# Hourglass attention then a quick-GELU layer on one Trainium2 core: GpSimd's order of work over v, q and k, two moves placed earlier, one load placed later

## The chip, the cores and the metric

The kernel runs on one core of one Trainium2 chip. The metric is the time of one execution on the device in microseconds (us). The engines are named as in the profile: PE (TensorE, matrix products; PEld is its weight load), DVE (VectorE), ACT (ScalarE), POOL (GpSimd) and SP (SyncE, which here only issues DMAs; POOL issues DMAs too). Each engine takes its own instructions strictly in order, and semaphores hold an instruction until what it needs is done.

## The reference, cut to what matters

Batch 8, 8 heads, 576 positions, head dimension 64. Two attentions are added: one over means of four neighbouring positions (its output is repeated four times), and one over the full sequence in which a position sees only positions less than 4 away. The result, as 4608 tokens of 512, goes through a 512 to 2048 to 512 layer.

```python
q_d = q.reshape(B, H, Sd, factor, D).mean(axis=3)      # factor = 4; k_d, v_d alike
out_up = np.repeat(sm_attn(q_d, k_d, v_d), factor, axis=2)
mask = np.abs(pos[:, None] - pos[None, :]) < factor
scores = np.where(mask, scale * np.matmul(q, k.transpose(0, 1, 3, 2)), -1e9)
out_local = np.matmul(softmax(scores), v)
x = (out_up + out_local).transpose(0, 2, 1, 3).reshape(B * S, H * D)
h = x @ w_in
return (h * (1.0 / (1.0 + np.exp(-1.702 * h)))) @ w_out
```

## The kernel before, in words

The order of every engine is written out by hand: an instruction stands on its engine where the Python code records it, and nothing reorders it. The main loop (line 1062) runs over 9 groups of 512 tokens. Group g computes the layer for its tokens: `mm1` (64 products at line 866 and a Silu on ACT at line 877), then `mm2` (64 products at line 930, output through `osb` at line 915). Into the same PE stream it weaves the attention of batch b = g + 1, whose result `xT` the next group reads. The places are counted in steps (line 959): a dictionary `steps` holds functions to call before a given product; steps 0 to 15 lie in `mm1`, step n from 16 on lies before product n - 16 of `mm2`. Functions with the same step run in the order in which they were added.

The heads of a batch are treated in two quads, qd 0 and 1. Per batch, in order:

- `load_qk` (line 201): POOL issues four DMAs, k and q of each quad, from float32 in memory to bfloat16 on chip. The buffers are double. `load_v` (ten DMAs from SP, float32, one buffer `vf`) and `load_v4` (twelve DMAs from SP into one buffer `v4`, four for each of three chunks) bring v in two layouts.
- `prep_qk` (line 298): DVE transposes k and q (line 270) into `kT` and `qT`. From batch 3 (`WIDE` = 3) on, the layout is turned so that 64 rows serve one head: `keep_odd` (line 278) has POOL copy the odd halves of k and q, and `swap` has DVE make eight moves for each quad (line 286, one 32 x 576 piece each): two that overwrite the odd half of k, two that put the kept half in its place, then the same for q. The names below: k even, k odd, q even, q odd, each two moves.
- `pool_qk` (line 316): POOL sums four neighbouring positions of k, then of q (lines 322 and 326) into `kdT` and `qdT`, for the coarse scores.
- `prep_v4` (line 342): POOL sums four neighbouring values of v, a pair of instructions (lines 346 and 349) for each of three chunks, into `vd`. `prep_vx` (line 334): POOL casts `vf` to `vb`, three instructions (lines 336 and 338).
- On PE: `s_pe(0)` at step 13 and `s1` at step 34 (local scores, line 455, then coarse scores, line 464; these read `kdT` and `qdT`), and the AV products of the quads (line 809, `av_t`) at steps 44 and 58, 13 or 14 products apart. AV writes the three PSUM tiles `PA`; `normalise_t` (line 813) then takes logarithms and exponentials of the denominators on ACT (lines 821, 822), multiplies on DVE into `xT` (lines 827, 842), and adds the coarse part: on POOL for quad 0, on DVE for quad 1 (both line 836).

The code that places all this for b >= 3 is lines 1096 to 1109, and the steps are lines 1117 to 1124. In program order of batch b >= 3, POOL has before the change: sums of quad 0's k and q, the odd copies of quad 1, `v4` chunk 0, sums of quad 1's k and q, `v4` chunks 1 and 2, the four loads of batch b + 2 (while b < 6), then, from the steps, the odd copies of quad 0 of batch b + 1, the two adds of line 836, and the three casts of `vf` for batch b + 1.

Of the kernel before, what the change touches and what calls it, by code (L numbers as in the profile page):

```python
# [19 lines left out]
def kernel(  # L20
# [9 lines left out]
    nc = tc.nc  # L30
    B, H, S, D = q.shape
    SD = S // 4
    HP = H // 2
    NQ = H // 4
# [5 lines left out]
    WIDE = 3  # L40
# [147 lines left out]
    def load_1(name, src, store, b, qd):  # L188
        t = ldp.tile(
            [128, 1152], BF16, name=f"{name}b{qd}", tag=f"{name}b{qd}", bufs=2  # L190
        )
        nc.gpsimd.dma_start(
            out=t,
            in_=bass.AP(
                tensor=src.tensor, offset=src[b, 4 * qd].offset,
                ap=[[1152, 128], [1, 1152]],
            ),
        )
        store[b, qd] = t

    def load_qk(b, qd):
        load_1("k", k, kf, b, qd)
        load_1("q", q, qf, b, qd)
# [17 lines left out]
    def load_vb(b, i):  # L221
        for par in range(2):
            nc.gpsimd.dma_start(  # L223
                out=vbs[b % 2][64 * par : 64 * par + 64, i, :, 0:D],
                in_=bass.AP(
                    tensor=v.tensor,
                    offset=v[b, 0].offset + (114 * i + KSTART[par]) * D,
                    ap=[[D, 64], [S * D, H], [1, D]],
                ),
            )  # L230

    def load_v4(b):
        for kc in range(3):
            for u in range(2):
                for qd in range(NQ):
                    nc.sync.dma_start(
                        out=v4[64 * u : 64 * u + 48, kc, 2 * qd : 2 * qd + 2],
                        in_=bass.AP(
                            tensor=v.tensor,
                            offset=v[b, 4 * qd + u].offset + kc * 48 * 4 * D,  # L240
                            ap=[[4 * D, 48], [(3 - 2 * u) * S * D, 2], [1, 4 * D]],
                        ),
                    )
# [10 lines left out]
    def load_w_out(c):  # L254
        nc.gpsimd.dma_start(
            out=w_out_bf[:, 4 * c : 4 * c + 4, :],
            in_=bass.AP(
                tensor=moe_w_out.tensor, offset=moe_w_out.offset + c * 512 * d_model,
                ap=[[d_model, 128], [128 * d_model, 4], [1, d_model]],
            ),  # L260
        )


    qT, kT, qdT = {}, {}, {}
# [11 lines left out]
    odd = {}  # L276

    def keep_odd(b, qd):
        for name, src in (("k", kT), ("q", qT)):
            t = work.tile([128, S], BF16, name="odd", tag="odd")  # L280
            nc.gpsimd.tensor_copy(out=t, in_=src[b, qd][:, :, 1])  # L281
            odd[name] = t

    def move(dst, src):
        with nc.allow_low_precision("a sum of one element each"):
            nc.vector.tensor_reduce(  # L286
                out=dst, in_=src[:, :, None], axis=mybir.AxisListType.X, op=ALU.add
            )

    def swap(b, qd):  # L290
        for name, src in (("k", kT), ("q", qT)):
            tt = src[b, qd]
            for p in (0, 64):
                move(tt[p : p + 32, :, 1], tt[p + 32 : p + 64, :, 0])
            for p in (0, 64):
                move(tt[p + 32 : p + 64, :, 0], odd[name][p : p + 32])

    def prep_qk(b, qd):
        prep_1("k", b, qd)
        prep_1("q", b, qd)  # L300
# [6 lines left out]
    def reduce_qk(b, qd, name):  # L307
        t = kdT[qd][:, 0:SD, :] if name == "k" else new_qdT(b, qd)
        src = (kT if name == "k" else qT)[b, qd]
        with nc.allow_low_precision("the sum is rounded once, as the pairwise one is"):  # L310
            nc.vector.tensor_reduce(
                out=t, in_=src.rearrange("p (j f) a -> p j a f", f=4),
                axis=mybir.AxisListType.X, op=ALU.add,
            )

    def pool_qk(b, qd, names="kq"):
        for name, src in (("k", kT), ("q", qT)):
            if name not in names:
                continue
            sv = src[b, qd].rearrange("p (j f) a -> p j f a", f=4)  # L320
            t1 = work.tile([128, SD, 2, 2], FP32, name="pq", tag="pq")
            nc.gpsimd.tensor_tensor(  # L322
                out=t1, in0=sv[:, :, 0:2, :], in1=sv[:, :, 2:4, :], op=ALU.add
            )
            dst = kdT[qd][:, 0:SD, :] if name == "k" else new_qdT(b, qd)
            nc.gpsimd.tensor_tensor(
                out=dst, in0=t1[:, :, 0, :], in1=t1[:, :, 1, :], op=ALU.add
            )
# [5 lines left out]
    def prep_vx(b):  # L334
        x, y = vf[b], vbs[b % 2]
        nc.gpsimd.tensor_copy(out=y[:, :, 0::2, 0:D], in_=x[:, :, 0::2])
        for p in (0, 64):
            nc.gpsimd.tensor_copy(
                out=y[p : p + 64, :, 1::2, 0:D], in_=x[64 - p : 128 - p, :, 1::2]
            )  # L340

    def prep_v4(b, eng, kcs=range(3)):
        for kc in kcs:
            x = v4[0:112, kc].rearrange("p h (f d) -> p h f d", f=4)
            t1 = work.tile([128, HP, 2, D], FP32, name="v2", tag="v2")
            eng.tensor_tensor(  # L346
                out=t1[0:112], in0=x[:, :, 0:2, :], in1=x[:, :, 2:4, :], op=ALU.add
            )
            eng.tensor_tensor(
                out=vds[b % 2][0:112, kc, :, 0:D],  # L350
                in0=t1[0:112, :, 0, :], in1=t1[0:112, :, 1, :], op=ALU.add,
            )


    def flat(p):
        return p.rearrange("p x n -> p (x n)")
# [516 lines left out]
    def new_gT():  # L873
        return moe_sb.tile([128, n_ffc, TG], BF16, name="gT", tag="gT")
# [90 lines left out]
    def after(src, eng):  # L965
        return lambda t: eng.tensor_copy(out=t, in_=src)
# [95 lines left out]
    for g in range(n_groups):  # L1062
        b = g + 1
        if g == 0:
            load_vb(1, 0)
            load_vb(1, 1)
            prep_qk(1, 0)
            pool_qk(1, 0)
            prep_qk(1, 1)
            load_vb(1, 2)  # L1070
            load_vb(1, 3)
            load_vb(1, 4)
            load_w_out(2)
            load_w_out(3)
            reduce_qk(1, 1, "q")
            reduce_qk(1, 1, "k")
            for qd in range(NQ):
                load_qk(2, qd)
            nc.gpsimd.memset(v4[32:64], 0.0)
            for x, c in ((0, 1.0), (1, 4.0)):  # L1080
                nc.vector.memset(ones[:, x, :], c)
            load_v(2, gate=after(w_out_bf[0:1, 12, 0:1], nc.gpsimd))
            load_v4(2)
        elif b < WIDE:
            for p in (0, 64):
                nc.vector.tensor_copy(out=mask[p : p + 64, 1], in_=mask[64 - p : 128 - p, 0])
            prep_qk(b, 0)
            pool_qk(b, 0)
            for qd in range(NQ):
                load_qk(b + 1, qd)  # L1090
            prep_vx(b)
            load_v(b + 1)
            prep_qk(b, 1)
            pool_qk(b, 1)
            prep_v4(b, nc.gpsimd)
        elif b < B:
            if b + 1 < B:
                load_v(b + 1)
            swap(b, 0)
            pool_qk(b, 0)  # L1100
            prep_qk(b, 1)
            keep_odd(b, 1)
            swap(b, 1)
            prep_v4(b, nc.gpsimd, (0,))
            pool_qk(b, 1)
            prep_v4(b, nc.gpsimd, (1, 2))
        if 1 < b < B - 2:
            for qd in range(NQ):
                load_qk(b + 2, qd)
        steps = {}  # L1110
        if b < B:
            pos = POS_G.get(g, POS)
            for n, f in zip(pos, attention(b, None if g else (1, 2))):
                steps.setdefault(n, []).append(f)
            if g == 0:
                steps.setdefault(VDP_0, []).append(lambda: prep_vd_pe(1, flat(PA[2])))
            if g and b + 1 < B:
                for n, f in (
                    (17, lambda: prep_qk(b + 1, 0)),
                    (17, lambda: keep_odd(b + 1, 0)),  # L1120
                    (45, lambda: prep_vx(b + 1)),
                    (32, lambda: load_v4(b + 1)),
                ):
                    steps.setdefault(n, []).append(f)
        gT = new_gT() if g else gT0
        mm1(g, gT, steps, 0 if g else 6)
        mm2(g, gT, {n - 16: f for n, f in steps.items() if n >= 16})
# [30 lines left out]
```

## Time and profile before

| quantity | value |
| --- | --- |
| median of 3 runs | 314.78 us (314.07 to 315.19) |
| the profiled execution's own time | 315.07 us |
| its span (first to last instruction) | 313.0 us, so 2.1 us lie outside it |
| PE busy | 295.1 us |
| DVE, ACT, POOL busy | 184.5, 208.9, 176.8 us |
| granted PE clock | full in every slice |
| group 2, first product to that of group 3 | 34.20 us |
| groups 3, 4, 5 | 32.28, 32.26, 32.28 us |
| group 6 | 32.59 us |

PE is the engine that is busy nearly all the time, so what counts is where it waits. A table of busy shares does not show that; the list of PE's waits and its timeline do. Groups 2 to 6 carry the batches (3 to 7) in the turned layout, which is where the change works. Times in the text are from the start of the span unless counted from a group's first product at line 866.

### The profile page before, as it was taken

The numbers are of one execution on the slowest core, as the hardware profiler recorded it, in microseconds if no ns is written. First come the engines' busy times: TensorE is split into PE (matmuls) and PEld (weight loads), VectorE is DVE, ScalarE is ACT, GpSimd is POOL, SyncE is SP. The second block draws the span as 40 slices with busy tenths as digits, with TensorE's granted clock in tenths as the row PEclk, the third lists the DMA queues.
The fourth block names the chain that finished last, engine by engine and source line by source line (L and its number), as shares of the span: only waits on it lengthen the run. The fifth ranks groups of instructions, "written<-read, shape, count | busy, mean of one in ns | idle before, by whom it ended". The sixth has DMA issues, their size and how long they took to land.

```text
span 313.0 us, 8666 instructions
## 1 busy us (share of the span) xinstructions
PE 295.1 (94%) x3620; PEld 148.9 (48%) x3663; DVE 184.5 (59%) x343; ACT 208.9 (67%) x349; POOL 176.8 (56%) x212
## 2 busy tenths in 40 slices
PE   7789999999999969998999999998999899999995
PEld 3455455445544435444544454445444544444444
DVE  5883526812787986997699869986996340000000
ACT  5556781867886767668866887688769686316611
POOL 8764690299829799379938894777577500000000
PEclk9999999999999999999999999999999999999999
DMA  6999999899799669823983299417100110010011
GB/s 133 155 197 209 172 118 208 164 197 276 153 233 229 133 149 215 205 42 99 208 233 70 74 201 246 89 49 174 68 2 35 38 67 2 34 67 36 0 67 67
DMA packets 64646, 40.01 MB, mean 128 GB/s; under 512 B 44640, under 2 KB 56032, under 8 KB 64608
## 3 DMA queue, kind: packets, MB, share of 16 engines
q0 software_dynamic: 18336, 14.81, 34.0%
q1 hardware_dynamic: 45600, 24.46, 30.2%
q8 instruction: 28, 0.46, 0.7%
q10 hardware_dynamic: 672, 0.20, 0.3%
q14 instruction: 10, 0.08, 0.1%
HBM read 44.83 MB, written 9.44 MB: 173 GB/s over the span
## 4 chain that ended last, share of the span: by engine, by line
PE 45%; DVE 23%; POOL 14%; issue 6%; ACT 5%; DMA 5%; SPq 1%; POOLq 0%; ACTq 0%
PE pm L930 18%; PE pm L866 15%; DVE kT L286 9%; DVE qT L286 9%; POOL v L346 5%; POOL pq L322 4%; PE pa L866 3%; PE pa L809 2%; DMA qb<-in_q_dram 2%; DVE xT L827 2%; ACT r L821 2%; ACT r L822 2%; PE pa L930 2%; DVE xT L836 2%; DMA vb<-in_v_dram 2%
## 5 line engine op out<-in xcount | busy, mean ns | idle before, releaser
L866 PE MATMUL pm<-xT,w_in_bf 128*128 128x512 bf16 x496 | 118.2, 379 | 1.6 <-ACT xT L669 0.5
L930 PE MATMUL pm<-w_out_bf,gT 128*128 128x512 bf16 x505 | 114.6, 379 | 3.3 <-issue 3.2
L877 ACT ACTIVATE gT<-pm 128x512 bf16<-128x512 f32 x128 | 76.3, 598 | 41.9 <-PE pm L866 41.9
L866 PEld LDWEIGHTS <-w_in_bf 128*128 128x128 bf16 x576 | 55.6, 98 | 67.2 <-issue 1.1
L930 PEld LDWEIGHTS <-gT 128*128 128x128 bf16 x560 | 52.8, 98 | 62.1 <-issue 0.5
L497 DVE TENSOR_TENSOR es<-es,mask 128x600 bf16<-128x600 bf16 x28 | 22.4, 820 | 25.6 <-ACT es L483 25.0
L827 DVE TENSOR_TENSOR xT<-pa,r 128x300 bf16<-128x300 f32 (+3 forms) x96 | 24.1, 304 | 21.3 <-ACT r L822 16.9
L915 ACT ACTIVATE osb<-pm 128x512 f32<-128x512 f32 (+2 forms) x35 | 20.2, 580 | 24.0 <-PE pm L930 18.4
L917 DVE TENSOR_SCALAR osb<-pm 128x128 f32<-128x128 f32 x1 | 0.3, 292 | 55.5 <-ACT osb L915 55.5
L322 POOL TENSOR_TENSOR pq<-kT 128x576 f32<-128x576 bf16 x13 | 14.9, 1146 | 28.3 <-DVE kT L286 18.0
L821 ACT ACTIVATE r<-pa 128x504 f32<-128x504 f32 (+1 forms) x36 | 20.6, 573 | 11.9 <-PE pa L809 11.9
L346 POOL TENSOR_TENSOR v<-v 112x512 f32<-112x512 f32 x18 | 24.5, 1359 | 0.0
L270 DVE STREAM_TRANSPOSE kT<-kb 128x576 f32<-128x576 f32 x16 | 20.0, 1252 | 6.0 <-DMA kb<-in_k_dram 5.8
L322 POOL TENSOR_TENSOR pq<-qT 128x576 f32<-128x576 bf16 x14 | 16.3, 1167 | 12.5 <-DVE qT L286 12.3
L483 ACT ACTIVATE es<-pa 128x600 bf16<-128x600 f32 x32 | 19.7, 668 | 5.1 <-PE pa L401 5.0
L822 ACT ACTIVATE r<-r 128x504 f32<-128x504 f32 (+1 forms) x36 | 22.2, 617 | 1.1
L270 DVE STREAM_TRANSPOSE qT<-qb 128x576 f32<-128x576 f32 x16 | 19.8, 1240 | 0.5 <-DMA qb<-in_q_dram 0.4
L866 PE MATMUL pa<-xT,w_in_bf 128*128 128x512 bf16 x63 | 19.6, 379 | 0.0
L286 DVE TENSOR_REDUCE kT<-kT 32x576 bf16<-32x576 bf16 x20 | 15.9, 793 | 3.5 <-POOL odd L281 3.1
L223 POOL DMA_DIRECT2D vb<-in_v_dram x18 | 12.3, 698 | 9.3 <-DMA w_in_bf<-in_moe_w_in_dram 4.2
L836 POOL TENSOR_TENSOR xT<-xT,ydt 128x576 bf16<-128x576 bf16 x12 | 13.9, 1187 | 5.8 <-DVE xT L827 5.8
L286 DVE TENSOR_REDUCE kT<-odd 32x576 bf16<-32x576 bf16 x20 | 15.9, 795 | 0.6
(119 smaller groups left out, 364.6 us busy)
## 6 DMA issues: line engine op xcount, KB each, us to landing
out_dram<-osb SPq DMA_DIRECT2D x35, 256.0 KB, 3.2
vf<-in_v_dram SPq DMA_DIRECT2D x61, 128.0 KB, 4.5
v<-in_v_dram SPq DMA_DIRECT2D x72, 96.0 KB, 3.9
kb<-in_k_dram POOLq DMA_DIRECT2D x16, 288.0 KB, 7.5
qb<-in_q_dram POOLq DMA_DIRECT2D x16, 288.0 KB, 9.3
w_in_bf<-in_moe_w_in_dram POOLq DMA_DIRECT2D x4, 512.0 KB, 7.2
w_out_bf<-in_moe_w_out_dram POOLq DMA_DIRECT2D x4, 512.0 KB, 12.5
vb<-in_v_dram POOLq DMA_DIRECT2D x18, 64.0 KB, 6.5
```

Source lines behind the costliest of these rows:

```text
L270: nc.vector.transpose(out=t32.rearrange("p (i c) -> p c i", c=18), in_=store[b, qd].bitcast(FP32).rearrange("p (c d) -> p c d", c=18),)
L286: nc.vector.tensor_reduce(out=dst, in_=src[:, :, None], axis=mybir.AxisListType.X, op=ALU.add)
L322: nc.gpsimd.tensor_tensor(out=t1, in0=sv[:, :, 0:2, :], in1=sv[:, :, 2:4, :], op=ALU.add)
L346: eng.tensor_tensor(out=t1[0:112], in0=x[:, :, 0:2, :], in1=x[:, :, 2:4, :], op=ALU.add)
L497: nc.vector.tensor_tensor(out=ev, in0=ev, in1=mask, op=ALU.mult)
L821: nc.scalar.activation(out=r, in_=den, func=AF.Ln)
L822: nc.scalar.activation(out=r, in_=r, func=AF.Exp, scale=-1.0)
L827: nc.vector.tensor_tensor(out=sub(x[u], t0 + at, (114, n), (1, c)), in0=sub(src, c0, (60, n), (1, c)), in1=sub(rc, c0, (60, n), (1, c)), o ...
L866: nc.tensor.matmul(acc, lhsT=w_in_bf[:, dmc, ffc * 128 : (ffc + 1) * 128], rhs=xT[dmc][:, g * TG : g * TG + TG], start=(dmc == 0), stop=(d ...
L877: nc.scalar.activation(out=gT[:, ffc, :], in_=acc, func=AF.Silu, scale=GELU_SCALE)
L915: eng.activation(out=osb, in_=ap, func=AF.Copy, scale=1.0 / GELU_SCALE)
L930: nc.tensor.matmul(ops[t], lhsT=gT[:, ffc, t * 128 : (t + 1) * 128], rhs=w_out_bf[:, ffc, :], start=(ffc == 0), stop=(ffc == n_ffc - 1),)
```

## The change

- The function `swap` becomes `swap_even` and `swap_odd`, for one of k and q and one quad. The DVE instructions are the same ones.
- The two k-even moves of quad 0 of batch b + 1 (b + 1 >= 3) are recorded at step 45 of group g, behind `normalise_t` of quad 0 and ahead of that of quad 1. The other six moves of quad 0 stay at the start of the next group. The eight of quad 1 keep their order.
- From batch 4 on, `prep_v4` of chunks 0 and 1 stands ahead of `pool_qk` of quad 0, and chunk 2 ahead of `pool_qk` of quad 1. For batch 3 chunks 0 and 1 stand ahead of `pool_qk` of quad 1 (before: chunk 0 alone) and chunk 2 behind it.
- `load_qk` of batch 4, which stood at the start of group 1's steps (behind `prep_v4` of batch 2), is recorded at step 45 behind `prep_vx` of batch 3. The loads of batches 5 to 7 keep their place at the end of the block, which now ends with the q sum of quad 1 (batch 3: with chunk 2).

```diff
-    def swap(b, qd):
-        for name, src in (("k", kT), ("q", qT)):
-            tt = src[b, qd]
-            for p in (0, 64):
-                move(tt[p : p + 32, :, 1], tt[p + 32 : p + 64, :, 0])
-            for p in (0, 64):
-                move(tt[p + 32 : p + 64, :, 0], odd[name][p : p + 32])
+    def swap_even(name, b, qd):
+        tt = (kT if name == "k" else qT)[b, qd]
+        for p in (0, 64):
+            move(tt[p : p + 32, :, 1], tt[p + 32 : p + 64, :, 0])
+
+    def swap_odd(name, b, qd):
+        tt = (kT if name == "k" else qT)[b, qd]
+        for p in (0, 64):
+            move(tt[p + 32 : p + 64, :, 0], odd[name][p : p + 32])
...
         elif b < B:
             if b + 1 < B:
                 load_v(b + 1)
-            swap(b, 0)
+            swap_odd("k", b, 0)
+            swap_even("q", b, 0)
+            swap_odd("q", b, 0)
+            if b > WIDE:
+                prep_v4(b, nc.gpsimd, (0, 1))
             pool_qk(b, 0)
             prep_qk(b, 1)
             keep_odd(b, 1)
-            swap(b, 1)
-            prep_v4(b, nc.gpsimd, (0,))
+            for name in "kq":
+                swap_even(name, b, 1)
+                swap_odd(name, b, 1)
+            prep_v4(b, nc.gpsimd, (2,) if b > WIDE else (0, 1))
             pool_qk(b, 1)
-            prep_v4(b, nc.gpsimd, (1, 2))
-        if 1 < b < B - 2:
-            for qd in range(NQ):
-                load_qk(b + 2, qd)
+            if b == WIDE:
+                prep_v4(b, nc.gpsimd, (2,))
+
+        def load_next(b):
+            for qd in range(NQ if b < B else 0):
+                load_qk(b, qd)
+
+        if b >= WIDE:
+            load_next(b + 2)
...
                     (17, lambda: prep_qk(b + 1, 0)),
                     (17, lambda: keep_odd(b + 1, 0)),
+                    (45, lambda: swap_even("k", b + 1, 0)),
                     (45, lambda: prep_vx(b + 1)),
+                    (45, lambda: load_next(b + 2 if b < WIDE else B)),
                     (32, lambda: load_v4(b + 1)),
```

## The prediction

> **What bounds the kernel now.** I read the page's busy shares first, then PE's list of waits over groups 1 to 6, then the timelines of PE, POOL and DVE around each wait.
>
> ```profile
> PE 295.1 (94%) x3620; PEld 148.9 (48%) x3663; DVE 184.5 (59%) x343; ACT 208.9 (67%) x349; POOL 176.8 (56%) x212
> ```
> ```profile
> PE pa L809 <- POOL vd L349: 3.2, 5, 1.0
> PE pm L930 <- issue: 2.9, 18, 0.2
> PE pa L464 <- POOL qdT L326: 1.3, 1, 1.3
> ```
> PE is the bound, and in these groups only three things stop it. The "issue" pieces (0.16 each) belong to changing products and stay. Two are waits for POOL: 3.2 in five pieces, once in each of groups 2 to 6, where the AV products of quad 0 wait for the last `vd`, and once 1.3 in group 2, where the coarse scores of quad 1 wait for `qdT`. That is 4.5 in all.
>
> PE in group 3 (its first product is at 124.71), then POOL in the same group:
>
> ```profile
> 146.79 0.30 PE L809 MATMUL pa<-ed,vd 48*64 48x144 bf16 x6
> 147.57 0.26 PE L809 MATMUL pa<-ed,vd 48*64 48x144 bf16 x4 [0.48 <-POOL vd L349]
> ```
> ```profile
> 122.14 2.61 POOL L338 CAST vb<-vf 64x1280 bf16<-64x1280 f32 x2
> 128.49 1.15 POOL L322 TENSOR_TENSOR pq<-kT 128x576 f32<-128x576 bf16 x1 [3.73 <-DVE kT L286]
> ...
> 131.70 1.15 POOL L322 TENSOR_TENSOR pq<-qT 128x576 f32<-128x576 bf16 x1 [1.32 <-DVE qT L286]
> ...
> 137.60 1.15 POOL L322 TENSOR_TENSOR pq<-kT 128x576 f32<-128x576 bf16 x1 [0.76 <-DVE kT L286]
> ...
> 140.89 1.15 POOL L322 TENSOR_TENSOR pq<-qT 128x576 f32<-128x576 bf16 x1 [1.40 <-DVE qT L286]
> 142.12 0.97 POOL L326 TENSOR_TENSOR qdT<-pq 128x288 bf16<-128x288 f32 x1
> 143.05 1.51 POOL L346 TENSOR_TENSOR v<-v 112x512 f32<-112x512 f32 x1
> ...
> 146.68 0.84 POOL L349 TENSOR_TENSOR vd<-v 112x256 bf16<-112x256 f32 x1
> ```
> POOL ends just too late, yet it stood idle for 3.73 + 1.32 + 0.76 + 1.40 = 7.2 in that group, always for DVE's moves, while `v4` chunks 1 and 2 were queued behind. The bound is this chain: DVE's moves, POOL's sums, two pairs for `v4`, PE. Each DVE pair of moves takes 1.6.
>
> Group 2 starts worse. POOL, then DVE:
>
> ```profile
> 93.50 1.25 POOL L336 CAST vb<-vf 128x1280 bf16<-128x1280 f32 x1 [6.15 <-DMA v<-in_v_dram]
> ```
> ```profile
> 101.90 1.63 DVE L286 TENSOR_REDUCE kT<-kT 32x576 bf16<-32x576 bf16 x2 [2.08 <-POOL odd L281]
> ```
> The casts for batch 3 wait 6.15 for `vf`, the odd copies come late, and DVE's moves of quad 1 with them.
>
> **The change, part by part.**
>
> *v4 earlier (groups 3 to 6).* Worked in group 3's time, 0 = its first product. The casts end at 0.0 (124.75) and DVE's last add at 0.4 (125.06). Chunks 0 and 1 now follow: a pair of lines 346 and 349 beside moves ran 134.77 to 136.85 = 2.1, so both end at 4.2. DVE does k odd, q even, q odd: three pairs of 1.65, ready at 2.0 and 5.3. POOL sums k from 4.2 to 6.1, q to 7.9 (1.85 each, 128.49 to 130.38), copies the odd halves (0.6 each) until 9.2, sums chunk 2 until 11.3. DVE, after two transposes of 1.1 (ends 7.6), waits for the k copy at 8.6 and moves k until 11.9, q until 15.2. POOL sums k, then q until 17.0. Before, `vd` was complete at 147.52 = 22.8 and PE needed it at about 22.3; now it is complete at 11.3. The wait goes: 3.2 minus group 2's 0.97 = 2.2. What is late next: `qdT` at 17.0, needed at 18.9 (143.64), so 1.9 in hand (0.5 before).
>
> *k-even moves between the AVs.* Two moves, 1.6, leave the start of the group (counted above) and stand on DVE ahead of quad 1's multiplies. They need POOL's odd copy of k: after the q sum (17.0) come the four load issues (to 19.2), and the copy, which also needs DVE's transpose of k (143.34 plus 1.25, so 19.9), ends near 20.5; the moves stand at 26.4 (151.1). If that copy were late, quad 1's multiplies would stand behind the moves; it has 5.9 in hand. Cover:
>
> ```profile
> 86.54 0.59 DVE L827 TENSOR_TENSOR xT<-pa,r 128x300 bf16<-128x300 f32 x2 [1.22 <-ACT r L822]
> ...
> 153.02 0.59 DVE L827 TENSOR_TENSOR xT<-pa,r 128x300 bf16<-128x300 f32 x2 [1.92 <-ACT r L822]
> ...
> 155.93 1.41 DVE L836 TENSOR_TENSOR xT<-xT,pa 128x576 bf16<-128x576 bf16 x2
> ...
> 158.28 0.38 PE L866 MATMUL pm<-xT,w_in_bf 128*128 128x512 bf16 x1
> ```
> DVE idles there 1.22 (group 1) or 1.92, of which 0.48 existed only because PE's second AV was held up; 1.44 stays. So the multiplies start 0.2 to 0.4 late. Behind them is the second add, ending at 157.34, and PE reads its result at 158.28: 0.94 in hand. I cost it at nothing. Without any cover: 1.65 less 0.19 of a later wait less 0.94 = 0.5 in each of groups 1 to 5, 2.6 in all; below nothing it cannot go, since its gain is counted in the chain.
>
> A closer second AV might meet DVE's reads of PSUM; group 1 already runs its AVs without that wait (80.45 and 84.66, and no wait between), so none is added.
>
> *Load of batch 4 behind the casts.* Four issues (0.55 each, 2.2) leave POOL at 80.35 and stand behind the casts. The view of line 212 in the stretch 79.3 to 83.5 reads:
>
> ```profile
> L212 SPq DMA_DIRECT2D vf<-in_v_dram x5: 636/817/4458, 79.3 to 83.1; - x5
> ...
> DMA to landing us min/median/max: 6.1/10.1/10.3
> ```
> against a median of 4.5 over the kernel: the last `vf` load, 83.09, landed 10.3 later, 93.4, which is when the casts began. Without that traffic the last one takes some 0.9 to issue and 4.5 to land: 88.5 (an estimate from these rows; ends 87.4, when POOL is free, and 93.4, no gain). Casts to 92.5, four issues to 94.7, k and q sums to 98.4, odd copies to 99.7, chunks 0 and 1 to 103.9; DVE's moves of quad 1 begin at 99.1, not 101.90, and end at 105.7; k and q sums then end at 107.6. Coarse scores could start near 109.4 (110.87 less 1.31, less a little): the wait of 1.3 goes. `vd` is complete at 109.7, needed near 113: the 0.97 goes too. The load itself, issued near 93, is needed by DVE at 110.22: 17 against landings of 5 to 13.
>
> On SP nothing moves. The loads of batches 5 to 7 are issued some 6 earlier than at 147.46, and now run beside `v4` of the next batch.
>
> **Sum.** 2.2 + 1.0 + 1.3 = 4.5 off 315.07, the profiled execution's own time (0.3 above the median): 310.6. By group lengths: 34.20 and 32.59 to about 31.8, three times 32.28 to 31.8, 4.7. I take 310.5.
>
> **The rivals.**
>
> *v4 comes too late (slower).* New: POOL stands for `v4` of the next batch already at that group's start, with the q and k sums and odd copies queued behind; before, it was needed 10 later. In group 3 the view of line 236 reads:
>
> ```profile
> L236 SPq DMA_DIRECT2D v<-in_v_dram x12: 375/428/1532, 144.4 to 151.4; - x12
> ...
> DMA to landing us min/median/max: 2.6/4.9/9.4
> ```
> Chunk 1's last load, the eighth, is issued near 149.4 = 24.7; with 4.9 to 6.0 (the median of the six issued beside q and k) it lands by 30.7, wanted when the casts end, near 32.1. It may come 1.9 later still before PE waits. At the worst landing, 9.4, PE loses 0.1; at the pace of the disturbed `vf` loads (1.52 each, 10.3 to land) chunk 1 lands at 42, and PE loses 8 in each of groups 3 to 5. It decides from about 35.5 on, where 1.5 in three groups eats the gain. At the `vf` pace with a median landing, 36.8: 2.8 each, 8.4: 319.0. Against: `v4` moves at its own pace in the trace even beside q and k. Chance 0.12.
>
> By the Trainium skill, DMA: Bandwidth & Descriptors, section Queues, rings and completion order, a DMA engine takes its queues in turn, one packet each, so a load cannot run ahead of others on another queue. By it `v4` ends only with the q and k loads, issued near 18 and landed 10.6 later at most in group 3: about 30, the same sum, but it speaks for this rival more than the row does.
>
> *Group 2 keeps its waits.* If `vf` still lands at 93.4, casts end 97.5, issues 99.7, sums 103.4, odd copies 104.7, chunks 0 and 1 108.9, `qdT` 112.5: PE waits 3.1 in place of 2.3. Gain 2.2 - 0.8 = 1.4: 313.7. For it: SP's issues were slow already at 72.33, before those loads. Chance 0.14.
>
> *The moves are not covered.* 310.6 + 2.6 = 313.2. Against: the idle 1.22 to 1.92 is in every group. Chance 0.06.
>
> **How the numbers follow.** The forecast has 0.68, the others 0.12, 0.14, 0.06. The low end is 314.78 less 4.7, less 0.3 for the runs' spread: 309.8. The upper end takes in the two weaker gains, 313.8, and leaves out the slower case. A measurement can tell about 0.3% (0.9 us) from no change. Faster: 0.68 + 0.06 + three quarters of 0.14 = 0.84, rounded to 0.83; same 0.05; slower 0.12.
>
> **What would show it.** Right: PE's waits for `vd` and `qdT` gone in groups 2 to 6, group lengths 31.8, casts of batch 3 near 88, POOL idle little before quad 0's k sum, DVE's moves standing behind line 827 of quad 0. Wrong: POOL at line 346 waiting for a DMA, PE at line 464 waiting for `qdT`, or PE at line 866 waiting for DVE's line 836.

## The result, and the profile after

The changed kernel took 310.33 us (median of 4 runs, 309.54 to 310.98) against 314.42 us for the kernel before in the same comparison (314.0 to 315.19): a ratio of 0.9866, with a 95% interval of 0.9834 to 0.9898. Forecast were 310.5 us, 309.8 to 313.8. The profiled execution took 310.23 us with a span of 308.4. Below, medians take in every run, while ratios leave out runs of a slower state at a lower clock, of which only moves4 had any (two of ten, 318.24 and 318.56; without them its median is 314.78).

The page of the changed kernel, busy shares and the chain that ended last:

```profile
PE 300.2 (97%) x3663; PEld 148.9 (48%) x3663; DVE 180.4 (58%) x343; ACT 208.6 (68%) x349; POOL 173.2 (56%) x212
...
PE 92%; DVE 2%; DMA 2%; ACT 1%; issue 1%; POOL 0%; DVEq 0%; ACTq 0%; POOLq 0%
```

The chain lay on DVE and POOL for 37% of the span before; now it is PE for 92%. PE's list of waits holds nothing between 78 and 260, and over the whole span only these, the last of them at group 1's first product:

```profile
PE pm L708 <- DVE wf L117: 1.7, 1, 1.7
PE pa L403 <- DVE qT L270: 1.0, 1, 1.0
PE pm L655 <- issue: 0.9, 1, 0.9
PE pa L419 <- DVE qdT L313: 0.3, 1, 0.3
PE pm L868 <- ACT xT L671: 0.3, 1, 0.3
PE pm L868 <- ACT osb L917: 0.2, 1, 0.2
```

Busy time by stage of the changed kernel, groups 2, 3 and 6 (length; then PE, PEld, DVE, ACT, POOL busy, granted clock, DMA share, GB/s). PE is busy for the whole of each:

```profile
91.65:123.25 31.60, 31.60 (x386) 15.42 (x385) 26.78 (x47) 24.79 (x41) 25.97 (x32) 1.00 0.95 185
123.25:154.83 31.58, 31.58 (x386) 15.42 (x385) 25.83 (x47) 24.78 (x40) 23.89 (x28) 1.00 0.69 152
...
217.98:249.55 31.57, 31.57 (x386) 15.41 (x385) 22.02 (x43) 24.78 (x40) 17.27 (x19) 1.00 0.09 36
```

Groups 2 to 6 took 34.20, 32.28, 32.26, 32.28, 32.59 before (163.6) and take 5 times about 31.58 (157.9): 5.7 less. The two profiled executions differ by 4.6 because the changed kernel's group 1 began 1.0 later (59.34 against 58.32) and took 0.1 longer; groups 7 and 8 together took the same 58.9.

POOL of the changed kernel in group 3, which begins at 123.24, and the product that needs the last of it:

```profile
121.33 2.61 POOL L340 CAST vb<-vf 64x1280 bf16<-64x1280 f32 x2
124.01 1.27 POOL L348 TENSOR_TENSOR v<-v 112x512 f32<-112x512 f32 x1
...
128.07 1.15 POOL L324 TENSOR_TENSOR pq<-kT 128x576 f32<-128x576 bf16 x1
...
134.33 0.73 POOL L351 TENSOR_TENSOR vd<-v 112x256 bf16<-112x256 f32 x1
135.81 1.15 POOL L324 TENSOR_TENSOR pq<-kT 128x576 f32<-128x576 bf16 x1 [0.75 <-DVE kT L286]
...
140.32 0.67 POOL L328 TENSOR_TENSOR qdT<-pq 128x288 bf16<-128x288 f32 x1
```
```profile
142.17 0.39 PE L466 MATMUL pa<-qdT,kdT 64*64 64x144 bf16 x12
```

The idle 3.73 and 1.32 ahead of quad 0's sums are filled by `v4`; `vd` is complete at 135.06, 11.8 after the group's first product (22.8 before), and `qdT` at 140.99, 1.2 before PE takes it.

The moves between the AVs on DVE of the changed kernel, in group 3:

```profile
149.66 1.61 DVE L286 TENSOR_REDUCE kT<-kT 32x576 bf16<-32x576 bf16 x2
151.28 0.59 DVE L829 TENSOR_TENSOR xT<-pa,r 128x300 bf16<-128x300 f32 x2
...
153.91 1.41 DVE L838 TENSOR_TENSOR xT<-xT,pa 128x576 bf16<-128x576 bf16 x2
```

They stand without a gap ahead of quad 1's multiplies; the last add ends at 155.32, 0.5 after the next group's first product (154.82), where PE wants it 1.3 after.

### The profile page after: what moved, and what is told of

Same layout as the page of the kernel before. It is cut to its first block, busy times and chain, and to the rows that moved or that the text cites. A ratio compares the mean times of both kernels' runs of the same rounds, so it can differ in the third digit from the quotient of the medians.

```text
span 308.4 us, 8705 instructions
## 1 busy us (share of the span) xinstructions
PE 300.2 (97%) x3663; PEld 148.9 (48%) x3663; DVE 180.4 (58%) x343; ACT 208.6 (68%) x349; POOL 173.2 (56%) x212
## 4 chain that ended last, share of the span: by engine, by line
PE 92%; DVE 2%; DMA 2%; ACT 1%; issue 1%; POOL 0%; DVEq 0%; ACTq 0%; POOLq 0%
PE pm L932 37%; PE pm L868 36%; PE pa L868 4%; PE pa L811 4%; DMA qb<-in_q_dram 2%; PE pa L932 2%; PE pa L457 1%; PE pm L947 1%; PE pa L419 1%; DVE qT L270 1%; PE pa L403 1%; PE pa L466 1%; ACT od L678 1%; PE pm L708 1%; DVE kT L270 0%
## 5 line engine op out<-in xcount | busy, mean ns | idle before, releaser
L932 PE MATMUL pm<-w_out_bf,gT 128*128 128x512 bf16 x528 | 119.2, 380 | 0.0
L499 DVE TENSOR_TENSOR es<-es,mask 128x600 bf16<-128x600 bf16 x28 | 18.6, 693 | 30.2 <-ACT es L485 29.9
L348 POOL TENSOR_TENSOR v<-v 112x512 f32<-112x512 f32 x18 | 23.0, 1279 | 0.3
```

Of the source, the lines that this page charges most:

```text
L348: eng.tensor_tensor(out=t1[0:112], in0=x[:, :, 0:2, :], in1=x[:, :, 2:4, :], op=ALU.add)
L932: nc.tensor.matmul(ops[t], lhsT=gT[:, ffc, t * 128 : (t + 1) * 128], rhs=w_out_bf[:, ffc, :], start=(ffc == 0), stop=(ffc == n_ffc - 1),)
```

## The experiments

The change has three parts, so six kernels leave one out or make one alone; two more press on the two margins (the time that DVE has for moves between the AVs, and the time in hand when `v4` lands); four repeat a profile. Times are medians, with the ratio to the kernel before in the same comparison. The changed kernel was measured beside a before of 314.42, the four from no_load to only_v4 beside 313.96, the last four beside 314.88.

| kernel | v sums | moves | load | us | ratio (95%) | group 2 | groups 3 to 5 | group 6 |
| --- | --- | --- | --- | --- | --- | --- | --- | --- |
| changed | new | new | new | 310.33 | 0.9866 (0.9834 to 0.9898) | 31.59 | 31.58 | 31.57 |
| no_load | new | new | old | 310.15 | 0.988 (0.9848 to 0.9912) | 32.65 | 31.58 | 31.58 |
| no_moves | new | old | new | 310.55 | 0.9891 (0.986 to 0.9923) | 31.58 | 31.58 | 31.58 |
| no_v4 | old | new | new | 310.44 | 0.989 (0.9849 to 0.9932) | 31.58 | 31.58 | 31.58 |
| only_v4 | new | old | old | 310.15 | 0.9878 (0.9844 to 0.9912) | 31.57 | 31.58 | 31.58 |
| only_moves | old | new | old | 311.71 | 0.9897 (0.9866 to 0.9928) | 31.57 | 31.58 | 31.58 |
| only_load | old | old | new | 314.03 | 0.9958 (0.9923 to 0.9993) | 32.27 | 32.28 | 32.61 |
| moves4 | new | four | new | 315.07 | 0.9996 (0.9968 to 1.0024) | 32.46 | 32.45 | 32.46 |
| v4_late | new | new | new | 319.77 | 1.0146 (1.0108 to 1.0183) | 31.58 | 34.99 | 33.80 |

(Group lengths are from one profiled execution each; groups 3 to 5 are a mean. That of v4_late took 321.22, 1.5 more than its median.)

**no_load.** The load of batch 4 goes back to its old place.

```diff
-        if b >= WIDE:
+        if b >= WIDE - 1:
             load_next(b + 2)
...
-                    (45, lambda: load_next(b + 2 if b < WIDE else B)),
```

> The changed kernel with the load of batch 4 back ahead of the odd copies in group 1. Theory one (the late vf costs group 2, and the other two edits absorb part of it): casts of batch 3 begin about 3 after group 2's first product, odd copies of quad 1 end at 11.9, chunks 0 and 1 at 16.1, the last qdT at 19.8 against 18.9 needed, so PE waits about 0.9 for qdT in group 2 and group 2 takes 32.5; groups 3 to 6 stay at 31.6; total about 311.2. Rival (the load's place is worth all of group 2's loss): group 2 back to 34.2, total 313. Rival (its place is worth nothing): 310.3, no wait.

Group 2 took 32.65, with the one wait of the forecast size; POOL's cast and PE's list of waits over groups 2 to 6:

```profile
93.27 1.25 POOL L338 CAST vb<-vf 128x1280 bf16<-128x1280 f32 x1 [5.79 <-DMA v<-in_v_dram]
```
```profile
PE pa L466 <- POOL qdT L328: 0.9, 1, 0.9
```

The casts began 2.6 after the group's first product, and 0.9 of that reached PE. Yet the times of the four runs (309.9 to 310.29) are no longer than the changed kernel's. That did not fit, and the repeats below say why.

**no_moves.** The two k-even moves go back to the start of the group.

```diff
-            swap_odd("k", b, 0)
+            swap_even("k", b, 0)
+            swap_odd("k", b, 0)
...
-                    (45, lambda: swap_even("k", b + 1, 0)),
```

> The changed kernel with the two k-even moves back at the start of the next group. Theory one (either of the two edits to POOL's and DVE's order is enough by itself in groups 3 to 6): DVE's eight moves of quad 0 end at 7.0 after the group's first product, POOL sums k until 6.7 and q until 8.9 behind chunks 0 and 1, the last qdT ends at 18.0 against 18.9, vd long before: no wait on PE, groups 2 to 6 at 31.6, total 310.3, but only 0.9 in hand. Rival (the moves are a needed part of the gain): a wait for qdT of 0.5 or more in each of groups 2 to 6, total 312.8 or more.

No wait on PE from group 2 on; `qdT` of quad 1 in group 3 ends at 141.96 and is taken at 142.52, so 0.6 is in hand and not 1.2. The moves buy a margin, not time.

**no_v4.** The v sums go back to their old order.

```diff
-            if b > WIDE:
-                prep_v4(b, nc.gpsimd, (0, 1))
...
-            prep_v4(b, nc.gpsimd, (2,) if b > WIDE else (0, 1))
+            prep_v4(b, nc.gpsimd, (0,))
             pool_qk(b, 1)
-            if b == WIDE:
-                prep_v4(b, nc.gpsimd, (2,))
+            prep_v4(b, nc.gpsimd, (1, 2))
```

> The changed kernel with the v sums in their old order (chunk 0 ahead of quad 1's sums, chunks 1 and 2 behind). Theory one (the moves alone shorten the chain by 1.65, more than the 0.5 to 1.0 that vd came late): vd complete near 21.0 after the group's first product against 22.3 needed, no wait on PE, groups 2 to 6 at 31.6, total 310.3. Rival (the order of the v sums is what removes the wait): vd waits of 0.5 in each of groups 3 to 6 stay, groups 3 to 5 at 32.2, total 312.5 to 313.

No wait again. In group 3 (first product at 124.40) POOL's last two chunks:

```profile
142.30 0.84 POOL L351 TENSOR_TENSOR vd<-v 112x256 bf16<-112x256 f32 x1
144.69 0.74 POOL L351 TENSOR_TENSOR vd<-v 112x256 bf16<-112x256 f32 x1
```

`vd` is complete 21.0 after the first product, as worked out: a chain shortened by 1.65 no longer reaches PE.

**only_v4 and only_moves.** The edits above combined, so that one part is left.

> The kernel before with the new order of the v sums alone. Theory one: groups 3 to 6 at 31.6 without a wait for vd; group 2, whose casts still begin near 3.0 after its first product, waits about 0.9 for qdT and takes 32.5; total about 311.2. Rival (the sums alone bring nothing, because POOL then comes late with the q and k sums): groups 3 to 6 stay at 32.2 with the wait at the coarse scores, total 314 or more.

> The kernel before with the two k-even moves alone placed between the AV products. Theory one: groups 3 to 6 lose their wait for vd (complete near 21.0 after the group's first product, needed at 22.3), 31.6 each; group 2 waits 0.9 for qdT and about 1 for vd, 33.5; total about 312.2. Rival (moves between the AVs delay quad 1's multiplies and take the gain back): PE waits for line 836's adds at the first products of groups 2 to 6, total 314 or more.

Groups 3 to 6 as theory one has them, 31.58 each: either part alone takes the whole wait. Group 2 was expected at 32.5 and 33.5 and took 31.57 in both. In only_v4 the casts began 1.1 after group 2's first product, in only_moves 3.2 before it, not 3.0 after.

**only_load.**

> The kernel before with the load of batch 4 alone placed behind the casts. Theory one: group 2 loses its qdT wait and becomes like group 3, 32.3 with a vd wait of about 0.5; groups 3 to 6 unchanged at 32.3 to 32.6; total 312.8 (315.0 less about 2). Rival (vf is late for another reason, SP's slow issue): casts of batch 3 still begin 3.0 after group 2's first product, total as before, 314.5.

PE's list of waits over groups 2 to 6:

```profile
PE pa L811 <- POOL vd L351: 2.7, 5, 0.8
PE pm L932 <- issue: 2.4, 15, 0.2
```

Group 2 became like group 3, 32.27, as theory one has it, and the others stayed at 32.3. The time moved by 0.4%, less than the 2 us expected.

**moves4.** The two q-even moves also go between the AVs.

```diff
-            swap_even("q", b, 0)
             swap_odd("q", b, 0)
...
                     (45, lambda: swap_even("k", b + 1, 0)),
+                    (45, lambda: swap_even("q", b + 1, 0)),
```

> The changed kernel with the two q-even moves of quad 0 also placed between the AV products. Tests the cover that the prediction set at 1.2 to 1.4 with 0.9 in hand behind it. Theory one: the first two moves have used the cover, so quad 1's multiplies start 1.65 later; DVE's second add ends 2.1 after the next group's first product where PE wants it at 1.3; PE waits 0.6 to 0.9 at line 868 (866 before) in groups 2 to 6; total about 314. Rival (there is more cover than the trace shows): no wait, 310.3.

PE's timeline at the start of groups 2 and 3, and DVE's last add before the second:

```profile
93.00 0.38 PE L868 MATMUL pm<-xT,w_in_bf 128*128 128x512 bf16 x1 [0.49 <-DVE xT L838]
...
125.46 0.38 PE L868 MATMUL pm<-xT,w_in_bf 128*128 128x512 bf16 x1 [0.49 <-DVE xT L838]
```
```profile
124.67 1.41 DVE L838 TENSOR_TENSOR xT<-xT,pa 128x576 bf16<-128x576 bf16 x2
```

Each group is 0.87 longer and the whole gain is gone. Two moves fit under the cover, four do not.

**v4_late.** The loads of `v4` are issued at step 72 in place of 32.

```diff
-                    (32, lambda: load_v4(b + 1)),
+                    (72, lambda: load_v4(b + 1)),
```

> The changed kernel with the twelve loads of v4 issued at step 72 (before product 56 of the second half) and not at step 32. Tests the price of the slower rival of the prediction. Theory one: chunk 1 lands near 38 after the group's first product, POOL ends both chunks about 3.6 later than now, 1.2 of it is in hand at the coarse scores, PE waits about 2.4 for qdT in each of groups 3 to 6: total about 320. Rival (POOL's and DVE's idle time absorbs it): 310.3 to 311.

POOL at its first sum of `v4` in group 3 (first product at 121.77), PE's list of waits over groups 2 to 6, PE's timeline in group 3, and the stages around it (columns as above, the third from the right is the granted clock):

```profile
125.58 1.26 POOL L348 TENSOR_TENSOR v<-v 112x512 f32<-112x512 f32 x1 [3.11 <-DMA v<-in_v_dram]
```
```profile
PE pa L466 <- POOL qdT L328: 7.3, 4, 1.8
```
```profile
143.16 0.39 PE L466 MATMUL pa<-qdT,kdT 64*64 64x144 bf16 x12 [1.84 <-POOL qdT L328]
143.70 3.62 PE L932 MATMUL pm<-w_out_bf,gT 128*128 128x512 bf16 x9 [0.16 <-issue]
```
```profile
143.00:144.00 1.00, 0.69 (x14) 0.50 (x15) 1.00 (x2) 0.41 (x1) 1.00 (x3) 1.00 0.06 16
144.00:145.00 1.00, 1.00 (x5) 0.33 (x4) 1.00 (x2) 0.48 (x1) 1.00 (x3) 0.56 0.66 56
145.00:146.00 1.00, 1.00 (x4) 0.45 (x3) 1.00 (x2) 0.00 (x0) 1.00 (x3) 0.50 0.92 168
```

319.77 against 320 expected. POOL stands 3.11 for the load of chunk 0, and PE waits for `qdT` behind it. The place and the order of the price were right (1.8 listed for each of four groups, 2.2 in the groups' length), but in the profiled execution part of it came from elsewhere: in groups 3 and 5 the clock fell to half after the wait, and those groups took 35.66 and 35.53, groups 4 and 6 33.77 and 33.80.

**Group 2, profiled again.** Two executions of the order of before (old_order_2, old_order_3: the instructions of before in their order), one more of only_moves, one more of no_load: 314.61, 314.21, 310.54 and 309.77 us, one run each, beside one of 313.54 of the kernel before.

> The order of before, profiled again, to see whether group 2's loss is the same in each execution. Theory two (the late vf is a race between vf's loads and the q/k loads, which the start-up decides): if group 1 begins near 58.5 the casts of batch 3 begin 1 to 3 after group 2's first product and group 2 takes 33 to 34.2; if the start-up had a stretch of low clock and group 1 begins after 60.5, the casts do not wait and group 2 takes 32.3. Rival (the loss belongs to the kernel): 34.2 each time.

> The order of before once more, for the same question. Theory two: casts 1 to 3 late and group 2 at 33 to 34.2 with a start of group 1 near 58.5, no wait and 32.3 with a start after 60.5. Rival: 34.2.

> The moves alone, profiled again. In the first run group 1 began at 60.8, the casts did not wait and group 2 took 31.6. Theory two: with a start near 58.5 the casts come 1 to 3 late and PE waits in group 2, 32.0 to 33.5; with a late start 31.6 again. Rival (the moves repair group 2 by themselves): 31.6 with either start.

> The changed kernel with batch 4's load at its old place, profiled again. In the first run the casts came 2.6 late and group 2 took 32.65. Theory two: 31.6 where the casts come less than about 2 late (or with a late start), up to 32.7 at 3 late. Rival: 32.65 each time.

The cast of batch 3 in old_order_2, then in old_order_3:

```profile
91.64 1.25 POOL L338 CAST vb<-vf 128x1280 bf16<-128x1280 f32 x1 [2.83 <-DMA v<-in_v_dram]
```
```profile
92.95 1.25 POOL L338 CAST vb<-vf 128x1280 bf16<-128x1280 f32 x1 [4.63 <-PE pa L868]
```

The second wait is listed under PE, but in that execution the last `vf` load went out at 81.77 and landed 10.9 later, at 92.7, just ahead of the cast.

| execution (load at its old place) | group 1 begins | `vf` loads out behind the first q or k load | casts after group 2's first product | group 2 |
| --- | --- | --- | --- | --- |
| before | 58.3 | 4 of 10 | 3.0 | 34.20 |
| no_load | 58.5 | 4 | 2.6 | 32.65 |
| only_v4 | 58.3 | 3 | 1.1 | 31.57 |
| no_load_2 | 58.9 | 1 | 0.1 | 31.58 |
| old_order_3 | 59.2 | 1 | 1.5 | 32.40 |
| only_moves_2 | 59.4 | 1 | 0.0 | 31.58 |
| old_order_2 | 59.6 | 1 | -0.3 | 32.27 |
| only_moves | 60.8 | 0 | -3.2 | 31.57 |

(The last column also depends on the other two parts of the change.)

How late `vf` comes belongs to the execution: in the order of before group 2 took 34.20 once, 32.27 and 32.40 the other times. Both theories put too much into it. The race itself can be read: the loads of q and k for batch 4 start 22.0 after group 1's first product in all eight, while the last `vf` load goes out at 81.5 to 83.1 of the span, whenever group 1 began. A `vf` load that went out behind the first of them landed 9.3 to 10.9 later (6.8 and 7.4 where it was less than 0.2 behind; the trace lacks two landings), one in the 3 us ahead 3.9 to 6.6. So a later group 1 leaves fewer `vf` loads behind, but a low clock in the start-up is not needed for it: old_order_2, only_moves_2 and no_load_2 had full clock from 20 to 30 and still came early enough. That `vf` comes late at all hangs on the place of the load: with the load behind the casts, the casts of batch 3 waited for no load in any of six profiles.

## Why the prediction was right, point by point

*The bound, and the waits that go.* Right: both waits are gone, and PE is the chain. What was mis-sized is how the sum is made. Groups 3 to 6 were put at 2.2, by the idle that the list of waits shows; by group length they gave 0.70, 0.68, 0.70 and 1.02, 3.1 in all. A wait listed at 0.48 cost 0.7, because products overlap and the idle is counted only from the end that the profile gives to the one ahead. The two products around the wait of group 3 before:

```profile
146.87 0.22 PE L809 MATMUL pa<-ed,vd 48*64 48x144 bf16 x1
147.57 0.26 PE L809 MATMUL pa<-ed,vd 48*64 48x144 bf16 x3 [0.48 <-POOL vd L349]
```

They begin 0.70 apart; in the changed kernel the same two begin 0.02 apart. The group lengths (4.7 in the same step, as a cross-check) were the better measure, though still 0.2 a group too long, since the length without a wait was got by taking 0.48 off.

*Group 2.* Put at 2.3. In the two profiled executions it was 2.6, but in both repeats the loss there was 0.7 to 0.8 (32.27, 32.40 against 31.58). So of the gain in the repeats, 3.8 to 3.9 by group lengths (161.7 and 161.8 against 157.9; 4.1 by the medians), group 2 gives 0.7 to 0.8, not half. That the total came out is in part luck: one term was read too large, from a single execution, and the other too small.

*The load behind the casts.* The mechanism was right: the casts waited for no `vf` (88.42, when POOL came free, in an execution that runs 1.1 later), and with the load at its old place in no_load 0.9 reached PE. That 88.42 meets the 88.5 of the estimate is chance: the estimate was for the landing of `vf`, whose last load went out at 82.16 and landed 3.7 later. (In the profile before, the last one landed 10.1 after its issue, at 93.2; 10.3 is the longest of the five.) The load's worth is small: only_load gained 0.4%, and no_load was not slower than the changed kernel. The rival that group 2 keeps its waits did not come.

*v4 earlier.* Right in the order; `vd` complete at 11.8 (11.3 worked out), `qdT` 17.75 (17.0), 1.2 in hand and not 1.9: the casts ended 0.7 after the group's first product and not with it. Not foreseen: the moves by themselves, 1.65, already exceed the 0.7 that the wait cost, so the two parts do the same work twice. The prediction added them in one chain and never asked what each gives alone.

*The moves.* Right: cost nothing, two fit, 0.8 is left behind them, and moves4 shows the price beyond, 0.87 a group. The cover was smaller than worked out: of the 1.92 idle not 0.48 but 0.70 hung on the held-up AV, and 1.22 stays, as DVE's idle there in only_v4 and no_moves shows. So the multiplies start 0.4 later, the upper end of the forecast, and the last add ends 0.15 later.

*v4 too late.* The rival's mechanism is real and its point right: v4_late lost 9 us by it (part of that, in the profile, by the clock). In the changed kernel it does not occur, though `v4` came later than the rows of before said. The view of line 236 in the changed kernel, group 3 (142 to 156):

```profile
L236 SPq DMA_DIRECT2D v<-in_v_dram x12: 311/506/1559, 142.9 to 154.5; - x12
DMA to landing us min/median/max: 2.5/8.0/8.8
```

The median rose from 4.9 to 8.0, since the q and k loads now run beside the first seven (in v4_late, from 120.9 to 125.0 and with those loads all but done, they landed in 2.6 to 3.2). Chunk 1's last load went out at 150.19 and landed 5.1 later, 32.0 after the first product where 30.7 was worked out, with 2.3 in hand before POOL took it. The Trainium skill, DMA: Bandwidth & Descriptors, Queues, rings and completion order, has each DMA engine serve its queues in turn, a packet at a time. The trace agrees in so far as the last q load, issued at 142.54, landed 8.9 later, at 28.2, and none of the seven `v4` loads issued beside it, which needed 7.9 to 8.8 each, landed ahead of it. That `v4` would end together with those loads was my inference and not the page's, and it did not: the eighth issue came 3.9 behind the seventh (150.19 against 146.25). SP's list of waits (140 to 156) has the reason, which the prediction did not look at:

```profile
SPq L236 <- DMA out_dram<-osb: 2.7, 1, 2.7
```

An output store issued on SP at 142.45 landed at 150.17, and SP held the eighth load until then.

*One wrong reading.* The "issue" pieces of 0.16 were said to belong to changing products. They are products missing from the record: only_moves shows 15 such pieces (2.4 in all) over groups 2 to 6 and no_v4 none, with groups of the same 31.58; the page counts 3620 PE products in the one and 3663 in the other. The same holds for before (3620) and the changed kernel (3663), so their PE busy times, 295.1 and 300.2, cannot be compared.

## What to carry to other kernels

Where an engine in order waits for something late while work with its inputs ready stands behind, put that work ahead; check first how long its own inputs take when everything else moves with it. When two edits shorten the same chain, work out what each gives alone: the second may buy only a margin. And take a stage's worth from its length, not from the idle that is listed, and in several executions: a loss that is seen in one profile may belong to that execution.

## What the runs showed of the hardware

In v4_late the wait of 1.84 on PE came four times, and after two of them, in groups 3 and 5, the granted clock stood at half for 3.41 us. Those groups took 35.66 and 35.53 against 33.77 and 33.80, so the same wait cost about 1.8 more. The two stretches begin at 144.13 and 212.39, which is 20 times 3.41 apart. Dividing the span at that pitch, these are the pieces that hold most of each wait (columns as above); the clock fell behind the first and the third, where PE was busy for 1.33 and 1.66 of 3.41, and not behind the others, with 1.86 and 1.89:

```profile
140.72:144.13 3.41, 1.33 (x53) 0.97 (x55) 3.38 (x5) 2.18 (x4) 3.23 (x4) 1.00 0.21 77
174.85:178.26 3.41, 1.86 (x46) 0.91 (x45) 3.35 (x5) 3.00 (x5) 1.96 (x2) 1.00 0.21 77
208.98:212.39 3.41, 1.66 (x45) 0.85 (x44) 3.35 (x5) 2.79 (x5) 2.07 (x2) 1.00 0.21 77
246.53:249.94 3.41, 1.89 (x19) 1.01 (x20) 2.02 (x3) 1.69 (x3) 1.23 (x2) 1.00 0.21 79
```

These are four cases of one execution, a reading and not a test. The Trainium skill, TensorE: Matmul & The Clock Gate, What's actually happening, puts the fall of the clock at an idle window of about 3.4 us and has the windows run free of the kernel. The trace agrees on the pitch (3.41), but here the window was not idle throughout: PE was busy for 1.33 and 1.66 of it.

The start-up can hold such a stretch too: in only_moves, only_load and no_v4 the granted clock from 20 to 30 was 0.83, at half for 3.41 of it, and group 1 began at 60.5 to 61.6, against 58.0 to 59.8 in the others, where it was full. What brings it on there is not shown. It moves the total by as much as a small edit.
